# w_out loaded eight rows to a partition, with strided weights for the d products and new transfer costs in the planner

## The chip, the cores and the metric

The kernel runs on one core of a Trainium2 chip. The metric is the device time of one execution in microseconds; lower is better. Times are medians over runs. A profile is one further execution, and its rows are microseconds from the first instruction unless marked ns.

## The reference

Eight sequences of 3072 tokens go through a gated attention without softmax, and its result goes through a layer with a maximum of two products:

```python
B, S, D = 8, 3072, 256        # z has 64 columns
scores = (z @ z.transpose(0, 2, 1)) / S
attn   = np.maximum(scores, 0.0) ** 2
x      = (u * (attn @ v)).reshape(B * S, D)
h1, h2 = x @ w1, x @ w2       # w1, w2: 256 x 1024
g      = np.maximum(h1, h2)
out    = g @ w_out            # w_out: 1024 x 256
```

All inputs and the output are float32. The kernel multiplies in bf16.

## The kernel before

**Algebra.** max(h1, h2) is written as relu(x(w1 - w2)) + x w2. So the kernel computes d = x(w1 - w2), then g = relu(d), and the output as g w_out + x (w2 w_out). The small product w2 w_out, called W2o, is made once on the chip: w2 is transposed by TensorE (job `w2t`, line 1593), copied, and multiplied with w_out (job `w2o`). w1 - w2 is made once by VectorE in w1's own tile (`w1_sb`).

**Steps.** A step is 512 tokens of one sequence, so there are 6 steps to a sequence and 48 in all. The first three are "plain"; the others use a seven-product scheme (after Strassen) for the attention times v (parts X and Y), for which sums of blocks (`es`) and of v (`lf`, the "folds") are formed on VectorE. For 44 of the steps the output product uses seven products too, with sums of w_out's blocks (`wf_sb`) and of g's (`gs`). Scores are symmetric: a block is computed once, and its other use gets it by a transposing DMA (`turn`, tile `aT`; within a diagonal group, inside `a_sb`). These are issued from SyncE's queue, as are the transposes of u (`uT`) and z (`zT`) and the stores. u, v, z and the weights are loaded, and cast to bf16, by DMAs from GpSimd's queue, each set to start when a named product has run ("timed load").

**TensorE's work.** Most products are "halved": a product over 128 rows is issued as two over 64 rows each, to the two halves of the array, which run side by side. One weight load (LDWEIGHTS) precedes each. A d part (`da`, `db`) is two pairs of halves, each with 512 columns of xT streaming past 128 columns of w1 as the weights. All matmuls go through one helper and show line 86. The 1024 columns of w1 are eight blocks of 128: block i gives rows of g that meet block i of w_out's rows. Which 128 columns make a block is free, as long as w1, w2 and w_out agree on it.

**Order.** The order of TensorE's instructions is written out by hand in a list (`work`), with the scores laid between. The orders of VectorE, ScalarE, SyncE and GpSimd, and the buffers that tiles share, come from a planner that runs when the kernel is built: a greedy simulation (`find_orders`) in which each job has a cost, and takes the engine when it is ready and due. It is repeated for 24 rounds, with margins added where TensorE would have waited, and the best round is kept. Nothing of the planner runs on the chip; a job that the plan puts too early on an in-order engine makes that engine wait.

**The planner's DMA.** A transfer starts 870 ns (SyncE) or 1770 ns (GpSimd) after its issue or when the queue is free, holds the queue for its cost in `DMA` times a factor, and lands some time later (`settle`). The factor is 1.1 before 100 us of the plan and 0.9 later. The time to land is 1330 ns, and 4000 ns after 125 us except for zT. The first loads have landing times of their own (`FIRST_LOADS`) and take no place in the queue. SyncE is taken for free again 1450 ns after an issue, or 4500 ns before the queue is free, if that is later.

Of the kernel before, what the change touches and what calls it, by code (L numbers as in the profile page):

```python
# [11 lines left out]
def kernel(  # L12
# [17 lines left out]
    nc = tc.nc  # L30
# [9 lines left out]
    P = 128  # L40
# [7 lines left out]
    KF = Dff // P  # L48
# [30 lines left out]
    pin = tc.keep_in_program_order  # L79
# [5 lines left out]
    def matmul(*args, **kw):  # L85
        newest[0] = pin(nc.tensor.matmul(*args, **kw)).ins  # L86
        for ins in fence:
            tc.add_manual_dep(newest[0], ins.name, SYNC, reason="a bank's other half of rows")
        fence.clear()
# [8 lines left out]
    def halved(half, out_ap, weights, moving, start, stop, **kw):  # L98
        rows = ds(half * 64, 64)
        matmul(out_ap, weights[rows], moving[rows], start=bool(start), stop=bool(stop), **kw)  # L100

    def sp_dma(**kw):
        pin(nc.sync.dma_start(**kw))


    def load(timed=False, **kw):
        dma = pin(nc.gpsimd.dma_start(**kw))
        if timed:
# [4 lines left out]
                reason="timed load",  # L113
            )

    def make_zT(z_sb):
        zT = zpool.tile([P, NSB + 1, P], bf16, name="zT")
        flat = z_sb.rearrange("p t d -> p (t d)")
        sp_dma(out=zT[:, 0 : NSB + 1 : 2, :], in_=flat, transpose=True)
        sp_dma(out=zT[:, 1 : NSB + 1 : 2, :], in_=flat[:, ds(dqk, NSB * dqk)], transpose=True)  # L120
        return zT
# [32 lines left out]
    w1_sb = consts.tile([P, KD, Dff], bf16)  # L154
    w_out_sb = consts.tile([P, KF, D], bf16)
# [7 lines left out]
    q = seqs[0]  # L163
# [6 lines left out]
    ident = consts.tile([P, P], bf16)  # L170
# [32 lines left out]
    RELU_BIAS, SQUARE_BIAS = 1200, -300  # L203
    TURN, TURN_LAG, UT_LAG = 1750, 4000, 7000

    DMA = dict(turn=1180, uT=1130, zT=4220, store=1940, v=1680, u=1680, z=3130, w1=4100, w2=3000, wo=4500)
    DMA_SMALL, DMA_PART, DMA_FULL, DMA_FULL_TO = 970, 0.9, 1.1, 100000
    DMA_START, DMA_END, DMA_LATE, DMA_AHEAD, SP_ISSUE = {"SP": 870, "POOL": 1770}, 1330, 4000, 4500, 1450
    FIRST_LOADS = {("v", 0, 0): 0, ("v", 0, 1): 1200, ("v", 0, 2): 2500, ("v", 0, 3): 3700, ("v", 0, 4): 4900, ("v", 0, 5): 7700, ("u", 0): 6300}

    class Job:
        def __init__(self, key, ways, fn, deps, new, uses, after, lag):
# [4 lines left out]
            self.due = 1e12  # L219
            self.dma = DMA.get(key[0], 0) if "SP" in ways or "POOL" in ways else 0  # L220
            if key[0] == "turn" and key[2] is None:
# [16 lines left out]
    def tile_of(pool, key):  # L238
        return bufs[pool, key].tile
# [520 lines left out]
    def acc_buf(i, key):  # L760
        buf(f"acc{i}", key, lambda: acc_psum.tile([P, GW], fp32, name=f"acc{i}"))
# [311 lines left out]
    def add_second(st, split):  # L1073
        n, b, c = st.n, st.b, st.s
# [16 lines left out]
        for i in range(KF // 2):  # L1091


            spare = (n, i) in SPARE_D
            turn_of = len(steps) + (SPARE_D.index((n, i)) if spare else 0)
            if spare:
                for j in range(2):
                    acc_buf(j, (turn_of, 0))
            banks = [(f"acc{j}", (turn_of, 0)) for j in range(2)] if spare else [("mm", ("d", n, i))]

            def bank(j, banks=banks):
                return tile_of(*banks[j]) if len(banks) > 1 else tile_of(*banks[0])[:, j, :]

            def products(_, i=i, bank=bank):
                for j in range(2):
                    for kc in range(KD):
                        matmul(
                            bank(j),
                            w1_sb[:, kc, ts(2 * i + j, P)],
                            tile_of(*xT)[:, :, kc, :],  # L1110
                            start=(kc == 0),
                            stop=(kc == KD - 1),
                        )

            def halves_of(part, i=i, bank=bank):
                if part:
                    fence.append(marks.pop(("d", n, i)))
                for kc in range(KD):
                    for half in range(2):
                        j = half ^ part  # L1120
                        halved(
                            half,
                            bank(j),
                            w1_sb[:, kc, ts(2 * i + j, P)],
                            tile_of(*xT)[:, :, kc, :],
                            start=kc == 0 and not part,
                            stop=kc == KD - 1 and part == 1,
                        )
                if not part:
                    marks["d", n, i] = mark()  # L1130

            d_key = ("d", n, i)
            if st.parted:
                d_key = ("db", n, i)
                job(
                    ("da", n, i),
                    {"PE": 430},
                    lambda _, f=halves_of: f(0),
                    deps=st.xT_jobs + [("w1-w2",)],
                    new=banks,  # L1140
                    uses=[xT] + banks,
                    lag=150,
                )
            job(
                d_key,
                {"PE": 430 if st.parted else 864},
                (lambda _, f=halves_of: f(1)) if st.parted else products,
                deps=st.xT_jobs + [("w1-w2",)],
                new=None if st.parted else banks,
                uses=[xT] + banks,  # L1150
                lag=150,
            )

            def do_relu(eng, i=i, banks=banks, bank=bank):
                if len(banks) > 1:
                    for j in range(2):
                        relu(eng, g_at(2 * i + j)[:, 0, :], bank(j))
                else:
                    relu(eng, g_at(2 * i, 2), tile_of(*banks[0]))

            job(
                ("g", n, i),
                {"ACT": 1000} if spare else {"DVE": RELU["DVE"]} if (n, i) == (last, KF // 2 - 1) else RELU,
                do_relu,
                deps=[d_key],
                new=gs[i // 2] if i % 2 == 0 else None,
                uses=[gs[i // 2]] + banks,
                after=[("g", n, 0)] if i else (),
            )
# [48 lines left out]
        for i in range(G // per):  # L1218
# [34 lines left out]
            if split:  # L1253
# [3 lines left out]
                    lambda _, i=i: sp_dma(out=out_b[:, c * G + i, :], in_=tile_of(*ok)[:, i, :]),  # L1257
# [123 lines left out]
    for name in "s20 a10 s21 b10 a11 a12 b11 a13 s22 b12 b13 s23 a00 a01 s10 b00 b01 s11 a02 a03 b02 b03 s12 o00 s13 o01 o02 o03".split():  # L1381
        n, i = last - int(name[1]), int(name[2])
# [68 lines left out]
    for n in range(PLAIN, len(steps)):  # L1451
        i = first_of[n]
# [12 lines left out]
    for w in reversed(range(len(windows))):  # L1465
        limit = min([limit] + [due[r] for r in windows[w] if r in due])
        found = [i for i in spots if begins[i] <= limit]
        i = found[-1] if found else 0
# [108 lines left out]
    W2, W2T = ("T", "w2"), ("T", "w2T")  # L1577
    bufs[W2] = Buf(lambda tag: widepool.tile([P, KD, Dff], bf16, name="w2_sb", tag=tag))
    bufs[W2T] = Buf(lambda tag: widepool.tile([P, KD, KF, P], bf16, name="w2T_sb", tag=tag))
    for tile_sb, source, key, at, new, rows in (  # L1580
        (lambda: tile_of(*W2), moe_w2, "w2", (0, 7), W2, "(c p) f -> p c f"),
        (lambda: w1_sb, moe_w1, "w1", (1, 2), None, "(c p) f -> p c f"),
        (lambda: w_out_sb, moe_w_out, "wo", (2, 2), None, "(c p) d -> p c d"),
    ):

        def fetch(_, tile_sb=tile_sb, source=source, rows=rows):
            load(timed=True, out=tile_sb(), in_=source.rearrange(rows, p=P))

        job((key,), {"POOL": 2000}, fetch, new=new, after=at_step(0, *at), lag=6500)
    def w2_transposes(_):  # L1590
        for dc in range(KD):
            for nb in range(KF):
                pin(nc.tensor.transpose(tile_of("mm", ("w2t", 0))[:, dc, nb, :], tile_of(*W2)[:, dc, ts(nb, P)], ident))  # L1593

    job(("w2t",), {"PE": 900}, w2_transposes, deps=[("w2",)], new=("mm", ("w2t", 0)), uses=[W2], lag=150)
    for dc in range(KD):
# [3 lines left out]
            lambda eng, dc=dc: copy(eng, tile_of(*W2T)[:, dc], tile_of("mm", ("w2t", 0))[:, dc]),  # L1600
# [36 lines left out]
    for dc in range(KD):  # L1637
# [3 lines left out]
            lambda eng, dc=dc: copy(eng, W2o_sb[:, dc, :], tile_of("mm", ("w2o", dc))[:, 0, :D]),  # L1641
# [9 lines left out]
    for args in plain_todo:  # L1651
        st, i, ks, dcs = args
# [126 lines left out]
    def find_orders():  # L1779
# [3 lines left out]
        dma_free = [10000]  # L1783
# [10 lines left out]
        def settle(j, begin, ns):  # L1794
            j.begin, j.done = begin, begin + ns + j.lag
            if j.key in FIRST_LOADS:
                j.done = FIRST_LOADS[j.key]
            elif j.dma:

                dma_free[0] = max(dma_free[0], begin + DMA_START["SP" if "SP" in j.ways else "POOL"]) + (DMA_FULL if begin < DMA_FULL_TO else DMA_PART) * j.dma  # L1800
                j.done = dma_free[0] + (DMA_LATE if begin > 125000 and j.key[0] != "zT" else DMA_END)
                if "SP" in j.ways:
                    idle_from["SP"] = max(begin + SP_ISSUE, dma_free[0] - DMA_AHEAD)
            for nxt, _ in j.succ:
                nxt.waits -= 1
                if not nxt.waits:
                    release(nxt)
# [21 lines left out]
        while len(emitted) < len(jobs) - len(HEAD_JOBS):  # L1829
            best = None  # L1830
            for e, todo in ready.items():
# [7 lines left out]
                at, _, j = min(found, key=lambda x: x[:2])  # L1839

                if e != "PE":
                    near = [x for x in found if x[0] <= at + PATIENCE]
                    at, _, j = min(near, key=lambda x: x[1] + WAIT_COST * (x[0] - at))
# [3 lines left out]
            at, e, j = best  # L1847
# [155 lines left out]
```

## Time and profile before

| what | value |
|---|---|
| median of 3 runs | 894.88 us (894.75 to 896.99) |
| profiled execution | 893.2 us, span 891.4 us |
| mean granted TensorE clock | 0.998 |
| TensorE busy | 882.7 us, 99% of the span |
| VectorE, ScalarE busy | 802.4 us (90%), 757.9 us (85%) |
| DMA moved | 146.17 MB, 164 GB/s on average |
| w_out's load, issue to landing | 8.5 us, 512 KB |

The profiled execution's time is its span and what lies around it. A matmul's end is modelled in the profile, so start-to-start distances are better than durations for what a product costs. In a row of the groups the columns are: line, engine, operation, output tile and input tiles, shape, count, then busy us, mean ns of one, and the engine's idle time before them with what ended it. In the order of time they are start, length, and the instruction; idle time before it stands in brackets.

### The profile page before, as it was taken

The numbers are of one execution on the slowest core, as the hardware profiler recorded it, in microseconds if no ns is written. First come the engines' busy times: TensorE is split into PE (matmuls) and PEld (weight loads), VectorE is DVE, ScalarE is ACT, GpSimd is POOL, SyncE is SP. The second block draws the span as 40 slices with busy tenths as digits, with TensorE's granted clock in tenths as the row PEclk, the third lists the DMA queues.
The fourth block names the chain that finished last, engine by engine and source line by source line (L and its number), as shares of the span: only waits on it lengthen the run. The fifth ranks groups of instructions, "written<-read, shape, count | busy, mean of one in ns | idle before, by whom it ended". The sixth has DMA issues, their size and how long they took to land.

```text
span 891.4 us, 37531 instructions
## 1 busy us (share of the span) xinstructions
PE 882.7 (99%) x16501; PEld 738.0 (83%) x16501; DVE 802.4 (90%) x1720; ACT 757.9 (85%) x952; POOL 59.8 (7%) x127
## 2 busy tenths in 40 slices
PE   9999999999999999999999999999999999999998
PEld 3368888878889988888888878888888898888886
DVE  6867799989999999999999999989998999989985
ACT  8867998879988999789997899978999799997634
POOL 3100000000000000000000000000000010000000
PEclk9999999999999999999999999999999999999999
DMA  9999999999999989999899999999999999996722
GB/s 160 171 167 148 188 199 160 179 188 187 157 163 169 193 151 174 170 179 203 121 169 173 191 184 143 169 166 213 150 148 172 187 199 158 136 199 115 128 58 73
DMA packets 380853, 146.17 MB, mean 164 GB/s; under 512 B 359184, under 2 KB 360848, under 8 KB 380688
## 3 DMA queue, kind: packets, MB, share of 16 engines
q1 hardware_dynamic: 364128, 114.01, 79.3%
q0 software_dynamic: 16560, 29.74, 23.3%
q8 instruction: 129, 2.11, 1.0%
q14 instruction: 36, 0.29, 0.1%
HBM read 59.77 MB, written 25.17 MB: 95 GB/s over the span
## 4 chain that ended last, share of the span: by engine, by line
PE 93%; ACT 3%; DMA 1%; DVE 1%; issue 1%; POOL 0%
PE acc L86 48%; PE s_ps L86 46%; ACT a_sb L282 1%; DMA aT<-a_sb 1%; ACT g_sb L282 1%; ACT o_sb L282 0%; DMA o_sb<-in_z_dram 0%; ACT g_last L282 0%; DVE gs L299 0%; DVE gs L296 0%; ACT a_sb L288 0%; ACT w2T_sb L293 0%; PE w2t_ps L1593 0%; DVE e L296 0%; DVE a_sb L290 0%
## 5 line engine op out<-in xcount | busy, mean ns | idle before, releaser
L86 PEld LDWEIGHTS <-v_sb 64*128 64x128 bf16 (+1 forms) x4464 | 332.4, 94 | 62.2 <-issue 8.4
L282 ACT ACTIVATE a_sb<-s_ps 128x1024 bf16<-128x1024 f32 (+1 forms) x335 | 302.3, 941 | 36.5 <-PE s_ps L86 33.6
L86 PEld LDWEIGHTS <-lf 64*128 64x128 bf16 x3240 | 264.2, 94 | 16.2 <-POOLq L94 3.2
L86 PE MATMUL acc<-es,v_sb 64*128 64x256 bf16 x2160 | 274.9, 269 | 0.0
L86 PE MATMUL acc<-es,lf 64*128 64x256 bf16 x1080 | 245.0, 269 | 0.0
L86 PE MATMUL acc<-a_sb,lf 64*128 64x256 bf16 x1224 | 232.1, 269 | 0.0
L86 PE MATMUL s_ps<-xT,w_sb 64*128 64x512 bf16 (+1 forms) x1504 | 212.6, 376 | 0.1
L288 ACT ACTIVATE a_sb<-a_sb 128x1024 bf16<-128x1024 bf16 (+1 forms) x224 | 209.9, 966 | 1.5
L282 ACT ACTIVATE g_sb<-s_ps 128x1024 bf16<-128x1024 f32 x187 | 186.0, 1024 | 14.0 <-PE s_ps L86 12.0
L86 PE MATMUL acc<-aT,lf 64*128 64x256 bf16 x936 | 177.5, 269 | 2.0 <-DMA aT<-a_sb 2.0
L86 PE MATMUL acc<-a_sb,v_sb 64*128 64x256 bf16 (+1 forms) x1344 | 140.2, 279 | 0.4 <-DVE xT L303 0.2
L86 PE MATMUL s_ps<-zT 64*128 64x512 bf16 (+2 forms) x774 | 120.2, 334 | 1.0 <-DVE zT L130 0.4
L86 PEld LDWEIGHTS <-gs 64*128 64x128 bf16 x2816 | 103.3, 94 | 9.9 <-issue 0.7
L296 DVE TENSOR_TENSOR es<-aT 128x1536 bf16<-128x1536 bf16 (+1 forms) x117 | 106.2, 931 | 0.5
L86 PEld LDWEIGHTS <-w_sb 64*128 64x128 bf16 (+1 forms) x1520 | 78.2, 94 | 25.5 <-POOLq L94 1.5
L86 PEld LDWEIGHTS <-g_sb 64*128 64x128 bf16 x2304 | 87.7, 94 | 10.4 <-POOLq L94 7.3
L290 DVE TENSOR_TENSOR a_sb<-a_sb 128x1024 bf16<-128x1024 bf16 (+1 forms) x112 | 72.2, 648 | 22.7 <-ACT a_sb L282 22.6
L86 PE MATMUL acc<-aT,v_sb 64*128 64x256 bf16 x936 | 86.8, 270 | 0.0
L299 DVE TENSOR_TENSOR es<-a_sb 128x512 bf16<-128x512 bf16 x198 | 79.4, 419 | 8.2 <-PE acc L86 8.0
L86 PE MATMUL s_ps<-wf_sb,gs 64*128 64x128 bf16 x2112 | 85.6, 217 | 0.0
L296 DVE TENSOR_TENSOR es<-a_sb 128x1024 bf16<-128x1024 bf16 x108 | 72.7, 684 | 0.0
L86 PE MATMUL s_ps<-w_out_sb,g_sb 64*128 64x128 bf16 (+1 forms) x1600 | 72.6, 222 | 0.0
(94 smaller groups left out, 1101.4 us busy)
## 6 DMA issues: line engine op xcount, KB each, us to landing
out_dram<-o_sb SPq DMA_DIRECT2D x47, 512.0 KB, 4.9
v_sb<-in_v_dram POOLq DMA_DIRECT2D x48, 256.0 KB, 5.8
u_sb<-in_u_dram POOLq DMA_DIRECT2D x48, 256.0 KB, 5.0
aT<-a_sb SPq DMA_TRANSPOSE x228, 5.1
z_sb<-in_z_dram POOLq DMA_DIRECT2D x7, 384.0 KB, 6.3
w_sb<-in_moe_w_dram POOLq DMA_DIRECT2D x2, 512.0 KB, 6.7
uT<-u_sb SPq DMA_TRANSPOSE x48, 5.2
a_sb<-a_sb SPq DMA_TRANSPOSE x45, 5.6
```

Of the source, the lines that this page charges most:

```text
L86: newest[0] = pin(nc.tensor.matmul(*args, **kw)).ins
L282: pin(nc.scalar.activation(out_ap, in_ap, AF.Relu))
L288: pin(nc.scalar.activation(ap, ap, AF.Square))
L290: pin(nc.vector.tensor_mul(ap, ap, ap))
L296: pin(nc.vector.tensor_add(*args))
L299: pin(nc.vector.tensor_sub(*args))
```

## The change

w_out's 1024 rows are dealt to the partitions differently: partition p gets rows 8p to 8p + 7, which lie one behind the other in memory, instead of row p of each block of 128. Block n of w_out then holds the rows 8q + n. So the columns of w1 and w2 that make block n are 8q + n too: the view `by_place` picks every eighth column, and the d products and the transposes of w2 read their weights with a step of 8 elements (16 bytes). Shapes, counts and order of the products stay.

In the planner, w_out's queue cost is 3000 ns instead of 4500. For jobs that begin between 31 and 56 us of the plan (from the third step into the fourth) the factor is 0.8 instead of 1.1, and the time to land 2800 ns instead of 1330. After 125 us, v's loads are reckoned to land 5500 ns after their queue time instead of 4000. The first transpose of u gets a landing time of its own, 13000 ns, and so takes no queue time in the plan.

```diff
+    def by_place(tile_sb):
+        return tile_sb.rearrange("p c (q n) -> p c n q", n=KF)
...
-    DMA = dict(turn=1180, uT=1130, zT=4220, store=1940, v=1680, u=1680, z=3130, w1=4100, w2=3000, wo=4500)
+    DMA = dict(turn=1180, uT=1130, zT=4220, store=1940, v=1680, u=1680, z=3130, w1=4100, w2=3000, wo=3000)
...
-    FIRST_LOADS = {..., ("v", 0, 5): 7700, ("u", 0): 6300}
+    FIRST_LOADS = {..., ("v", 0, 5): 7700, ("u", 0): 6300, ("uT", 0): 13000}
...
                         matmul(
                             bank(j),
-                            w1_sb[:, kc, ts(2 * i + j, P)],
+                            by_place(w1_sb)[:, kc, 2 * i + j, :],
...
                         halved(
                             half,
                             bank(j),
-                            w1_sb[:, kc, ts(2 * i + j, P)],
+                            by_place(w1_sb)[:, kc, 2 * i + j, :],
...
-        (lambda: w_out_sb, moe_w_out, "wo", (2, 2), None, "(c p) d -> p c d"),
+        (lambda: w_out_sb, moe_w_out, "wo", (2, 2), None, "(p c) d -> p c d"),
...
-                pin(nc.tensor.transpose(tile_of("mm", ("w2t", 0))[:, dc, nb, :], tile_of(*W2)[:, dc, ts(nb, P)], ident))
+                pin(nc.tensor.transpose(tile_of("mm", ("w2t", 0))[:, dc, nb, :], by_place(tile_of(*W2))[:, dc, nb, :], ident))
...
-                dma_free[0] = max(dma_free[0], begin + DMA_START["SP" if "SP" in j.ways else "POOL"]) + (DMA_FULL if begin < DMA_FULL_TO else DMA_PART) * j.dma
-                j.done = dma_free[0] + (DMA_LATE if begin > 125000 and j.key[0] != "zT" else DMA_END)
+                dma_free[0] = max(dma_free[0], begin + DMA_START["SP" if "SP" in j.ways else "POOL"]) + (0.8 if 31000 < begin < 56000 else DMA_FULL if begin < DMA_FULL_TO else DMA_PART) * j.dma
+                j.done = dma_free[0] + (DMA_LATE + 1500 * (j.key[0] == "v") if begin > 125000 and j.key[0] != "zT" else 2800 if 31000 < begin < 56000 else DMA_END)
```

More of the change, by code (lines that the diff above doesn't have):

```diff
@@ L204 @@
     TURN, TURN_LAG, UT_LAG = 1750, 4000, 7000
-    DMA = dict(turn=1180, uT=1130, zT=4220, store=1940, v=1680, u=1680, z=3130, w1=4100, w2=3000, wo=4500)
+    DMA = dict(turn=1180, uT=1130, zT=4220, store=1940, v=1680, u=1680, z=3130, w1=4100, w2=3000, wo=3000)
     DMA_SMALL, DMA_PART, DMA_FULL, DMA_FULL_TO = 970, 0.9, 1.1, 100000
     DMA_START, DMA_END, DMA_LATE, DMA_AHEAD, SP_ISSUE = {"SP": 870, "POOL": 1770}, 1330, 4000, 4500, 1450
-    FIRST_LOADS = {("v", 0, 0): 0, ("v", 0, 1): 1200, ("v", 0, 2): 2500, ("v", 0, 3): 3700, ("v", 0, 4): 4900, ("v", 0, 5): 7700, ("u", 0): 6300}
+    FIRST_LOADS = {("v", 0, 0): 0, ("v", 0, 1): 1200, ("v", 0, 2): 2500, ("v", 0, 3): 3700, ("v", 0, 4): 4900, ("v", 0, 5): 7700, ("u", 0): 6300, ("uT", 0): 13000}
     class Job:
```

## The prediction

> **What bounds the kernel now.** I read the page first, for which engine sets the end.
>
> ```profile
> span 891.4 us, 37531 instructions
> PE 882.7 (99%) x16501; PEld 738.0 (83%) x16501; DVE 802.4 (90%) x1720; ACT 757.9 (85%) x952; POOL 59.8 (7%) x127
> PE 93%; ACT 3%; DMA 1%; DVE 1%; issue 1%; POOL 0%
> ```
>
> TensorE is busy for 99% of the span and holds 93% of the chain that ended last. A change that leaves its instructions as they are can only win back time in which TensorE waits or runs slowly. The waits of TensorE alone, and the windows by ten microseconds, say how much of that there is. In the waits the columns are the sum, the number and the longest; the other entries of TensorE's list are under 0.5 us each and lie before 24 us.
>
> ```profile
> PE acc L86 <- DMA aT<-a_sb: 2.0, 1, 2.0
> PE zeros L86 <- DVE blank L166: 1.2, 1, 1.2
> ```
>
> The windows list each engine's busy time, then the granted clock, the DMA share and GB/s.
>
> ```profile
> 180.00:190.00 10.00, 9.02 (x182) 8.02 (x178) 9.76 (x19) 8.58 (x12) 0.53 (x1) 1.00 1.32 173
> 190.00:200.00 10.00, 9.01 (x156) 7.72 (x157) 5.92 (x13) 6.38 (x9) 0.53 (x1) 0.83 1.15 214
> ```
>
> Behind the first two microseconds there is one wait worth naming: a transposed tile (aT) came late once, by 2.0 us. In the window behind it the granted clock is 0.83 instead of 1.00. So (1 - 0.83) x 10 = 1.7 us more went to a slow clock. The order of time shows both, and the chain shows what they did to the step.
>
> ```profile
> 176.21 0.24 PE L86 MATMUL s_ps<-xf_sb,xs 64*128 64x128 bf16 x2
> 190.99 0.29 PE L86 MATMUL acc<-aT,lf 64*128 64x256 bf16 x2 [1.97 <-DMA aT<-a_sb]
> 192.47 0.35 PE L86 MATMUL s_ps<-xf_sb,xs 64*128 64x128 bf16 x2
> ```
>
> The chain, as start, length and what ran:
>
> ```profile
> 175.03 2.84 PE s_ps L86 x56
> 182.68 8.27 DMA aT<-a_sb
> 196.76 2.84 PE s_ps L86 x56
> 286.72 2.84 PE s_ps L86 x56
> 304.66 2.84 PE s_ps L86 x56
> ```
>
> From 175.03 to 196.76 this step of the second sequence takes 21.73 us. The same step of the third, from 286.72 to 304.66, takes 17.94. The difference, 3.79 us, is 1.97 us of waiting, about 1.7 of slow clock and 0.1 of rest: the same product lasts 0.24 us before and 0.35 after. By the Trainium skill (TensorE: Matmul & The Clock Gate, HAM oscillation), idle gaps matter only above about 3.4 us; by that rule the stall would be worth 1.97 us and its end would give 892.9 us. The trace disagrees, a gap of 1.97 us was followed by the clock of 0.83, so this rule gets no chance of its own.
>
> I take 3.79 us for the whole stall.
>
> Why was that tile late? First SyncE's queue (start, length of the issue), then the DMA issues of 172 to 182 us and of 287 to 300 us, with the median time to landing.
>
> ```profile
> 153.48 13.19 SPq L103 DMA_TRANSPOSE aT<-a_sb  x6
> 177.89 1.57 SPq L103 DMA_TRANSPOSE aT<-a_sb  x1
> 179.56 3.03 SPq L103 DMA_TRANSPOSE a_sb<-a_sb  x1
> 182.68 5.71 SPq L103 DMA_TRANSPOSE aT<-a_sb  x2
> 288.60 4.15 SPq L103 DMA_TRANSPOSE aT<-a_sb  x2
> ```
>
> ```profile
> aT<-a_sb SPq DMA_TRANSPOSE x2, 9.4
> v_sb<-in_v_dram POOLq DMA_DIRECT2D x2, 256.0 KB, 8.6
> aT<-a_sb SPq DMA_TRANSPOSE x4, 6.3
> v_sb<-in_v_dram POOLq DMA_DIRECT2D x1, 256.0 KB, 4.8
> ```
>
> From 153.48 on six transposes are issued without a pause, in 13.19 us. The two issued from 182.68 have their counterpart in the third sequence at 288.60. Counted from the step's start it is 7.65 us there (182.68 - 175.03) against 1.88 (288.60 - 286.72): here the queue is 5.8 us further behind. Transfers also land later: of those issued in 172 to 182 us aT takes 9.4 us and v 8.6, in 287 to 300 us 6.3 and 4.8. The transposes ahead in the queue cost 1.57 and 3.03 us each to issue. The stall is 2.0 us deep, so one place in this queue makes or ends it.
>
> **The change part by part.** *w_out's load.* The first row below is of the two loads of w1 and w2, the second of w_out's load; then the rows of that load and its readers.
>
> ```profile
> DMA to landing us min/median/max: 6.1/6.7/7.2
> w_out_sb<-in_moe_w_out_dram POOLq DMA_DIRECT2D x1, 512.0 KB, 8.5
> 40.67 0.92 POOL L107 DMA_DIRECT2D w_out_sb<-in_moe_w_out_dram  x1 [12.55 <-PE acc L86]
> 55.17 1.95 PE L86 MATMUL s_ps<-w_out_sb,w2T_sb 128*128 128x256 bf16 x16
> L296 DVE TENSOR_TENSOR wf_sb<-w_out_sb x1: 418/418/418, 56.3 to 56.3; 128x512 bf16<-128x512 bf16 x1
> ```
>
> It moves the same 512 KB in 8 KB runs instead of 1 KB runs. w1 and w2 have the same size and runs of 4 KB; they land in 6.7 us against 8.5. I take 6.7 for the changed load (bounds 6.1 and 8.5; longer than 8.5 is excluded, as the longer runs of w1 and w2 are faster). It lands about 47.4 instead of 40.67 + 8.5 = 49.2. Its first reader on TensorE starts at 55.17, its first on VectorE at 56.3, so 6 us of slack hide both values: 0 us on the path. With the cover gone, it would be worth 1.8 us. The transfers behind it in the queue (u at 41.58, the transposes, z) gain up to the same 1.8 us; TensorE's list of waits has none between 24 and 189 us, so that too is 0 at that place. The wf sums and all products keep their shapes: 0.
>
> *Strided weights.* The d products read w1 with a step of 8 elements (16 bytes) between columns; so do the 16 transposes of w2. By the code every weight load of the kernel before reads neighbouring columns, so no row shows this price, and it needs bounds.
>
> ```profile
> L86 PEld LDWEIGHTS <-w_sb 64*128 64x128 bf16 x1504 | 76.7, 94 | 23.5 <-POOLq L94 1.5 <-issue 0.6
> 175.99 0.40 PE L86 MATMUL s_ps<-wf_sb,gs 64*128 64x128 bf16 x8
> 176.83 1.04 PE L86 MATMUL s_ps<-xT,w_sb 64*128 64x512 bf16 x8
> 177.69 0.27 PE L86 MATMUL acc<-es,v_sb 64*128 64x256 bf16 x1
> 50.45 1.06 PE L1593 MATMUL w2t_ps<-ident,w_sb 128*128 128x128 bf16 x16
> 51.34 3.94 PE L86 MATMUL s_ps<-xT,w_sb 128*128 128x512 bf16 x16
> ```
>
> Eight products of 128 columns run from 175.99 to 176.21: 4 pairs in 0.22 us, 55 ns a pair. Each pair has two weight loads of its own, so two loads take at most 55 ns of the engine, whatever the 94 ns of a single record. A d pair streams 512 columns: from 176.83 to 177.69, 4 pairs in 0.86 us, 215 ns. Inside d the loads may become 215 / 55 = 3.9 times as long before anything waits. The thin place is the first pair of a d part that follows an output part, whose pairs cover only 55 ns: by the order of work that is 3 places in each of 44 steps, 132. At a double load each shows up to 55 ns: 132 x 55 ns = 7.3 us. The 16 transposes, at (51.34 - 50.45) / 16 = 56 ns each, add at most 0.9 us. Over 3.9 times as long, d itself would wait as well; no row points there, and the range leaves it out. Bounds: 0 and 8.2 us; a gain is excluded, since the loads of today already show nothing to win. I take 0, because the row it is nearest to is d's own, with its 160 ns of spare cover.
>
> The Trainium skill has rules for both sides. SBUF — State Buffer (Door 1, the note on cachelines) gives lines of 16 bytes and a price for each access to a new line; with this step every weight is on a new line, which speaks for the 7.3 us. TensorE: Matmul & The Clock Gate (Weight-path perf modes) lets the fast weight load take steps up to 1,024 elements, which speaks for 0. No run here shows either.
>
> *The plan's numbers.* TensorE's order comes from the list of work and is not touched. GpSimd's loads hang on products of that order and stay where they are. The orders of VectorE, ScalarE and SyncE, and which tile takes which buffer, come from the plan, and it reckons anew. The plan's zero is the first product.
>
> ```profile
> 7.69 1.02 PE L86 MATMUL acc<-a_sb,v_sb 128*128 128x512 bf16 x4
> aT<-a_sb SPq DMA_TRANSPOSE x228, 5.1
> 181.46 0.42 DVE L296 TENSOR_TENSOR lf<-v_sb 128x512 bf16<-128x512 bf16 x1
> 173.59 0.53 POOL L107 DMA_DIRECT2D v_sb<-in_v_dram  x1 [3.01 <-PE s_ps L86]
> ```
>
> So 31 to 56 us of the plan is 38.7 to 63.7 in the trace. There w_out was reckoned at 1770 + 1.1 x 4500 + 1330 = 8050 ns and becomes 1770 + 0.8 x 3000 + 2800 = 6970; a transpose goes from 870 + 1.1 x 1180 + 1330 = 3498 to 870 + 944 + 2800 = 4614, nearer to the 5.1 us of the trace. The queue is believed free 2550 ns earlier behind w_out and 354 ns earlier per transpose, so SyncE's order may differ from there on. After 125 us of the plan (133 in the trace) a v load goes from 1770 + 0.9 x 1680 + 4000 = 7282 to 8782 ns. The measured 8.6 us of the stalled stretch is nearer to the new number. It matters there: the first fold of v starts at 181.46, 7.87 us after its load was issued at 173.59 and in front of squares, on which transposes wait. The four folds (0.42 us each, 1.7 us together) move behind such work. New waits are not added to the code; an instruction placed too late holds up all behind it on its in-order engine, and TensorE then waits for an es or aT tile.
>
> The sum: w_out 0, strided loads 0, head of the kernel 0 (written by hand, unchanged), the stall -3.79. The profiled execution takes 893.2 us (its span and 1.8 around it) and would take 889.4; the median of the runs, 894.88, lies 1.7 above it and gives 894.88 - 3.79 = 891.1.
>
> **The rivals.** *A, the stall goes* (forecast): 891.1. For it: only 2.0 us of lateness, one place in SyncE's queue; both reckonings come nearer to what landed, the one for v just in this stretch. Against: the transposes ahead of the late one are probably ready earlier in any order.
>
> *B, the stall stays as it is*: 894.9. For it: SyncE issues without a pause for long before 182.68, so the 1.8 us saved at 49 us may be used up on the way.
>
> *C, another order, one more late tile*: DMA share is above 1 in the windows shown, so the queue has no spare time; if a plan with less queue time puts one more transpose (1.57 to 3.03 us of issue) ahead of one that is due, TensorE gets a second stall like this one. Price 3.79: 894.88 + 3.79 = 898.7. It decides as soon as the second tile is late by some tenths of a us.
>
> *D, strided loads show*: 894.88 + 7.3 = 902.2, 898.4 if the stall goes as well. It decides when two loads take over 55 + 2700 / 132 = 75 ns.
>
> **How the numbers follow.** A 0.52, B 0.16, C 0.20, D 0.12. About 0.3% (2.7 us) is what a measurement can tell from no change, so A is faster, B the same, C and D slower: 0.52, 0.16, 0.32. A's own range is 889.0 (the stall worth 1.7 us more in the runs that weren't profiled, and some tenths) to 892.2. The range over the cases is 889.0 to 901.0: it takes in A, B and C, and leaves out D's upper part, C with two more stalls and a little below, under 0.2 in all.
>
> **What would show it.** A: TensorE's waits without the 2.0 us for aT, a clock of 1.00 in 190 to 200 us, 17.9 us for that step. w_out's landing near 6.7 us, and TensorE contiguous from 40 to 58 us. Strided loads: 4 d pairs still in 0.86 us; 0.22 us more at the first pair after an output part would be D. C: a new entry "DMA aT" or "DVE es" in TensorE's waits and another window with a clock under 1.00. The forecast is wrong if the wait at 189 us is there still, or if one like it stands elsewhere.

## The result, and the profile after

The change makes the kernel slower: 900.95 us (median of 21, 894.24 to 905.56) against 894.59 before (median of 21, 891.85 to 900.04). The ratio is 1.0053, with a 95% interval of 1.0030 to 1.0077. That is half a percent. Measured three times more, the same kernel gave 1.0017 (0.9995 to 1.0039), 1.0031 (0.9992 to 1.0070) and 1.0053 (1.0026 to 1.0079); two of these intervals contain 1. The ratios leave out slow executions, those over 1.5% above the fastest of their kernel, while medians and counts here take all (without the slow ones the two counts below are 22 of 58 and 22 of 175).

The median hides the shape. The 21 times lie in two groups: ten from 894.24 to 896.79, with mean clocks of 0.999 to 1.000, and eleven from 900.95 to 905.56, with 0.996 to 0.998. I draw the line at 899 us and count the executions above it; in later measurements the two groups run into each other there (e16 has times of 898.24 and 899.61). Over all the measurements told of here they are 22 of 58 for the changed kernel and 24 of 177 for the kernel before (its single execution e12 not counted). So there are two questions: what makes an execution fall above the line, and what the lower group costs.

The profiled execution of the changed kernel took 895.05 us and fell in the lower group. Its page:

```profile
span 893.2 us, 37530 instructions
PE 884.3 (99%) x16501; PEld 766.2 (86%) x16501; DVE 800.8 (90%) x1719; ACT 759.4 (85%) x953; POOL 59.4 (7%) x127
PE 92%; ACT 4%; DVE 2%; issue 1%; DMA 1%; POOL 0%; POOLq 0%
```

TensorE still sets the end. Its instructions are as many as before; the weight loads (PEld) are busy for 28 us longer. The waits of TensorE (sum, number, longest; "issue" is a wait for which the profile shows no cause):

```profile
PE acc L86 <- issue: 1.3, 3, 0.5
PE zeros L86 <- DVE blank L169: 1.2, 1, 1.2
PE tpz_c L132 <- DMA z_sb<-in_z_dram: 0.6, 1, 0.6
PE s_ps L86 <- issue: 0.3, 1, 0.3
PE s_ps L86 <- DVE o_sb L299: 0.3, 1, 0.3
```

The windows that answer to the stall of before (busy time of each engine, granted clock, DMA share, GB/s):

```profile
180.00:190.00 10.00, 10.00 (x199) 9.73 (x196) 9.46 (x20) 9.21 (x12) 0.83 (x2) 1.00 1.29 209
190.00:200.00 10.00, 10.00 (x199) 9.51 (x196) 9.47 (x22) 9.26 (x15) 1.29 (x3) 1.00 1.06 174
```

The wait for aT is gone, TensorE is full from 180 to 200 us, and the clock is 1.00 throughout. That is what case A asked for, and the span is still 1.8 us longer than in the profile of before. The kernel before, profiled a second time (e12: 892.24 us, span 890.4, clock 1.000), shows why nothing was won:

```profile
180.00:190.00 10.00, 10.00 (x200) 9.13 (x197) 9.65 (x20) 9.21 (x11) 0.53 (x1) 1.00 1.27 216
190.00:200.00 10.00, 10.00 (x202) 8.87 (x198) 9.53 (x22) 9.41 (x15) 1.58 (x3) 1.00 1.09 188
```

The stall at 189 us isn't there either, and e1, which has the orders of before, doesn't have it (its longest wait is 1.5 us, at 735 us). It belonged to one execution of the kernel before, not to the kernel. Nor does its absence show in full: the span of e12 is only 1.0 us shorter than that of the profile with the stall. Among other things, e12 has 2.1 us of "issue" waits that the other has not.

**Where an upper execution loses.** One profile of the changed kernel fell above the line (904.58 us, span 902.7; experiment e16). The two longest waits of TensorE in it, behind the head:

```profile
PE acc L86 <- DMA a_sb<-a_sb: 6.0, 1, 6.0
PE acc L86 <- DVE e L299: 0.9, 1, 0.9
```

The windows around the first:

```profile
55.00:60.00 5.00, 4.08 (x49) 3.03 (x48) 2.04 (x5) 2.64 (x5) 0.53 (x1) 1.00 1.61 74
60.00:65.00 5.00, 0.00 (x0) 0.00 (x0) 0.00 (x0) 0.00 (x0) 0.00 (x0) 0.79 1.04 148
65.00:70.00 5.00, 4.90 (x50) 4.08 (x50) 3.59 (x12) 0.00 (x0) 0.00 (x0) 0.52 1.26 187
```

TensorE stands still for 6.0 us at 59 to 65 us, until the transposed diagonal tile of the fourth step (`turn` 3) lands. The five microseconds behind that run at 0.52 of the clock, worth (1 - 0.52) x 5 = 2.4 us. With the 0.9 us for e this is 9.3 of the 9.5 us by which its span exceeds the 893.2 of the lower execution.

**How it got there.** SyncE's queue (start, length of the issue) in the kernel before:

```profile
34.01 1.39 SPq L103 DMA_TRANSPOSE uT<-u_sb  x1
46.21 1.21 SPq L103 DMA_TRANSPOSE a_sb<-a_sb  x1
66.95 3.85 SPq L103 DMA_TRANSPOSE a_sb<-a_sb  x1
```

in the lower profile of the changed kernel:

```profile
36.97 1.29 SPq L103 DMA_TRANSPOSE uT<-u_sb  x1
39.54 10.24 SPq L103 DMA_TRANSPOSE aT<-a_sb  x4
49.88 1.43 SPq L103 DMA_TRANSPOSE a_sb<-a_sb  x1
73.97 1.24 SPq L103 DMA_TRANSPOSE a_sb<-a_sb  x1
```

and in the upper one:

```profile
38.38 1.29 SPq L103 DMA_TRANSPOSE uT<-u_sb  x1
39.76 13.72 SPq L103 DMA_TRANSPOSE aT<-a_sb  x4
53.58 4.51 SPq L103 DMA_TRANSPOSE a_sb<-a_sb  x1
```

The new plan puts transposes that are due later in front: `turn` 1-16 and 1-18 ahead of the third step's uT, 2-16 and 2-18 as well ahead of the diagonal tile, and seven more ahead of the next diagonal tile (`turn` 4). The first diagonal tile is issued at 49.88 instead of 46.21, the second at 73.97 instead of 66.95. With quick transfers that is early enough. In the upper execution the four transposes ahead take 13.72 us to issue instead of 10.24, and the tile itself takes 11.5 us to land instead of 5.2. The length of an issue holds its waiting too. The longest wait of SyncE's queue from 39 to 54 us, first in the upper execution, then its wait for TensorE in the lower one:

```profile
SPq L103 <- PE acc L86: 7.0, 1, 7.0
SPq L103 <- PE s_ps L86: 4.2, 1, 4.2
```

Both belong to `turn` 2-16, one of the transposes put in front: it isn't ready to go, and the diagonal tile stands behind it. The DMA issues of 40 to 64 us (median us to landing) in the lower profile:

```profile
w_out_sb<-in_moe_w_out_dram POOLq DMA_DIRECT2D x1, 512.0 KB, 6.3
u_sb<-in_u_dram POOLq DMA_DIRECT2D x2, 256.0 KB, 7.1
a_sb<-a_sb SPq DMA_TRANSPOSE x1, 5.2
```

and in the upper one:

```profile
w_out_sb<-in_moe_w_out_dram POOLq DMA_DIRECT2D x1, 512.0 KB, 9.2
u_sb<-in_u_dram POOLq DMA_DIRECT2D x2, 256.0 KB, 9.4
a_sb<-a_sb SPq DMA_TRANSPOSE x1, 11.5
```

Program and data are the same in both; what differs from execution to execution is how fast the early transfers land.

In the kernel before, the same tile lands no faster:

```profile
a_sb<-a_sb SPq DMA_TRANSPOSE x1, 10.2
```

It takes 10.2 us there, 10.4 in e12 and 12.3 in e4, and it is in time each time, because it is issued at 46.21 to 46.81: in e4 TensorE has no wait over 0.2 us from 24 to 100 us. Against the profile of before the upper execution issues the tile 7.4 us later (53.58 against 46.21), and its landing takes only 1.3 us more.

### The profile page after: what moved, and what is told of

Read it like the earlier page. It is cut to its first block, busy times and chain, and to the rows that moved or that the text cites. A ratio compares the mean times of both kernels' runs of the same rounds, so it can differ in the third digit from the quotient of the medians.

```text
span 893.2 us, 37530 instructions
## 1 busy us (share of the span) xinstructions
PE 884.3 (99%) x16501; PEld 766.2 (86%) x16501; DVE 800.8 (90%) x1719; ACT 759.4 (85%) x953; POOL 59.4 (7%) x127
## 4 chain that ended last, share of the span: by engine, by line
PE 92%; ACT 4%; DVE 2%; issue 1%; DMA 1%; POOL 0%; POOLq 0%
PE acc L86 47%; PE s_ps L86 45%; ACT a_sb L285 1%; ACT g_sb L285 1%; ACT a_sb L291 1%; DMA z_sb<-in_z_dram 1%; ACT o_sb L285 0%; DVE lf L302 0%; ACT e L820 0%; DVE o_sb L299 0%; DVE es L302 0%; DVE a_sb L293 0%; DVE o_sb L302 0%; DVE gs L302 0%; DVE gs L299 0%
## 5 line engine op out<-in xcount | busy, mean ns | idle before, releaser
L86 PEld LDWEIGHTS <-v_sb 64*128 64x128 bf16 (+1 forms) x4464 | 336.8, 94 | 58.0 <-issue 9.5
L86 PEld LDWEIGHTS <-lf 64*128 64x128 bf16 x3240 | 268.0, 94 | 14.1 <-DVE lf L302 1.2
L86 PE MATMUL s_ps<-xT,w_sb 64*128 64x512 bf16 (+1 forms) x1504 | 217.0, 378 | 0.2
L291 ACT ACTIVATE a_sb<-a_sb 128x1024 bf16<-128x1024 bf16 x225 | 210.9, 966 | 1.6
L86 PE MATMUL acc<-aT,lf 64*128 64x256 bf16 x936 | 179.4, 269 | 0.5 <-issue 0.5
L86 PE MATMUL s_ps<-zT 64*128 64x512 bf16 (+2 forms) x774 | 123.4, 333 | 1.0 <-DVE o_sb L299 0.3
L86 PEld LDWEIGHTS <-w_sb 64*128 64x128 bf16 (+1 forms) x1520 | 107.6, 142 | 12.9 <-issue 0.7
```

The lines of the kernel that those rows point to most:

```text
L291: pin(nc.scalar.activation(ap, ap, AF.Square))
```

## The experiments

Each ratio is to the kernel before, measured beside it on the same chip, with its 95% interval. "Plan" means the planner's numbers, "layout" the new w_out with the strided weights.

**The change taken apart: e1, e2, e3, e4.** e1 is the layout with the planner's numbers of before. e2 is the planner's numbers with the old layout. e3 is the whole change again. e4 is the kernel before with one of the numbers:

```diff
-                j.done = dma_free[0] + (DMA_LATE if begin > 125000 and j.key[0] != "zT" else DMA_END)
+                j.done = dma_free[0] + (DMA_LATE + 1500 * (j.key[0] == "v") if begin > 125000 and j.key[0] != "zT" else DMA_END)
```

> The layout alone (w_out eight rows to a partition, strided weights), with all planner numbers of before, so the orders of all engines are those of before. Theory O (the new orders make a tile late in part of the executions): 894.6 + 129 d parts behind an output part x 7.5 ns = 895.6 us, the wait of 2.0 us for aT at 189 us still there, times in one group. Theory W (strided weight loads cost the time): about 900 us as with the whole change.

> The planner numbers alone, with w_out in blocks of 128 rows and weights of neighbouring columns as before. Theory O: two groups of times as with the whole change, one near 893 to 895 us and one near 902 to 905 us, since the orders are those of the change. Theory W: 890 to 892 us, the stall at 189 us gone and nothing in its place.

> The whole change once more. Both theories: two groups of times, near 895 and near 903 us. If the profiled execution falls in the upper group: theory O expects one or two waits of TensorE of 2 us or more for an aT or es tile, each followed by a granted clock under 1.00; theory W expects no such wait but longer d parts.

> The kernel before with one number changed: v's loads after 125 us of the plan land 1500 ns later in the plan. Theory O with v's number as the cause: the wait at 189 us gone, 891 us in a lower group, and an upper group 8 us above it. Theory O with the early numbers as the cause: about 894.6 us, one group. Theory W: 891 to 895 us.

Measured: e1 893.38 us (0.9997, 0.9981 to 1.0012), none of 12 above 899. e2 901.50 (1.0066, 1.0035 to 1.0097), 8 of 12. e3 896.22 (1.0017), 2 of 13. e4 895.43 (1.0007, 0.9989 to 1.0026), none of 12. So the plan's orders make the loss, and neither the layout nor the later v does. No run changes another of the planner's numbers alone, so which of them moves the transposes stays open. Beside each other on one chip, the plan alone does worse than the whole change (e2 8 of 12, e3 2 of 13 above 899; over all runs 18 of 24 and 22 of 58). With the old layout w_out took 8.5 us or more to land in every profile, with the new one 6.2 to 7.1 in the quick ones, so the faster load may give back some lead; that isn't shown. e3's profile (906.45 us) fell above the line, at another place than e16's. Its waits from 44 to 72 us:

```profile
ACT w2T_sb L296 <- DVE w2T_sb L296: 10.9, 1, 10.9
PE s_ps L86 <- ACT w2T_sb L296: 10.1, 1, 10.1
DVE xT L306 <- DMA uT<-u_sb: 8.8, 1, 8.8
```

SyncE's issue of the third step's uT, as start and length:

```profile
51.06 5.45 SPq L103 DMA_TRANSPOSE uT<-u_sb  x1
```

The loads of w1 and of the third step's u (issues of 29.2 to 34 us, with the us to landing):

```profile
w_sb<-in_moe_w_dram POOLq DMA_DIRECT2D x1, 512.0 KB, 16.2
u_sb<-in_u_dram POOLq DMA_DIRECT2D x1, 256.0 KB, 17.0
```

The longest wait of SyncE's queue from 39 to 52 us:

```profile
SPq L103 <- DVE a_sb L293: 8.0, 1, 8.0
```

And the windows:

```profile
60.00:65.00 5.00, 0.00 (x0) 0.00 (x0) 2.71 (x6) 0.79 (x1) 0.00 (x0) 0.50 1.12 213
65.00:70.00 5.00, 4.72 (x22) 2.58 (x22) 4.90 (x13) 4.34 (x6) 0.00 (x0) 0.66 0.94 181
```

w1 took 16.2 us to land and the third step's u 17.0. That u was issued at 29.39, so it was there at 46.4. Its uT was issued at 51.06 only, instead of 36.97: in front of it stand `turn` 1-16 and 1-18, and the first of them waited 8.0 us for a tile of VectorE, which had itself waited 3.4 us for an aT that landed late. Late transfers and the new order work together here. VectorE waits 8.8 us for uT with the product xT. VectorE is in order, so its copy of w2T stands behind. ScalarE waits for that copy, and TensorE for ScalarE's. In the window behind, the clock is 0.66.

**Two transposes forward or back: e5 to e8.** Theory Q: the third step's uT and the diagonal tile of the fourth, put behind transposes that are not due, make the upper group. e5 is the plan again. e6 and e7 are plan and whole change with these two in front again; e8 is the kernel before with the two moved back.

```diff
+    put_behind(('uT', 2), [('turn', 1, 16), ('turn', 1, 18)])             # e6, e7
+    put_behind(('turn', 3, None), [('turn', 2, 16), ('turn', 2, 18)])
...
+    put_behind(('turn', 2, 12), [('uT', 2)])                              # e8
+    put_behind(('turn', 2, 18), [('turn', 3, None)])
```

> The planner numbers alone once more, as the measure of this call. Both theories: about 901 us, two thirds of the executions over 899 us.

> The planner numbers alone, and in SyncE's queue two urgent transposes taken back in front of two that are not: uT of the third step before turn (1,16) and (1,18), and the diagonal turn of the fourth step before turn (2,16) and (2,18). Nothing else of the orders changes. Theory Q (these two places in the queue make the upper group): about 894 us, hardly an execution over 899 us. Theory R (another part of the new orders, such as VectorE's folds that wait for v, makes it): 900 us or more, as without the edit.

> The whole change with the same two transposes taken back in front. Theory Q: 894 to 895 us, no execution over 899 us. Theory R: 896 to 901 us with a tenth to a half of the executions over 900 us, as for the whole change.

> The kernel before with the two transposes moved back in SyncE's queue: uT of the third step behind turn (1,16) and (2,12), the diagonal turn of the fourth step behind uT of that step and turn (1,18), (2,16) and (2,18). Theory Q: an upper group near 900 to 906 us appears, median 897 to 903 us. Theory R: 894.5 us as before.

Measured: e5 901.14 us (1.0058, 1.0020 to 1.0096), 10 of 12 above 899. e6 894.33 (1.0024, 0.9983 to 1.0065), 4 of 12. e7 902.08 (1.0061, 1.0024 to 1.0098), 7 of 12. e8 899.52 (1.0058, 1.0027 to 1.0089), 8 of 12. Moving the two back is enough to spoil the kernel before. Moving them forward helps the plan (4 of 12 against 10 of 12 in e5) and doesn't help the whole change (e7). The profile of e8 (903.47 us) has the stall of e3: TensorE waits 8.2 us at 54 us, through w2T, for the third step's uT. The profile of e7 (waits of TensorE) shows what was left there:

```profile
PE s_ps L86 <- ACT w2T_sb L296: 5.2, 1, 5.2
PE acc L86 <- DMA a_sb<-a_sb: 4.6, 1, 4.6
```

The first is the third step's uT again, which stands in front now, but waits for its u (12.8 us to land) and then takes 15.1 us itself. The second wait ends at 95.7 us, at the second diagonal tile, which the new plan also puts back and which I hadn't moved.

**The whole early queue: e9 to e12.** Theory Q2: all of SyncE's early order counts. e9 is the whole change a third time. e10 is the whole change with the first 32 issues of SyncE in the order of before. e11 is the layout with `turn` 0-18 and 1-16 put behind the diagonal tile. e12 is one profiled execution of the kernel before.

```diff
+    lines["SP"] = [named[k] for k in queue_of_before] + [x for x in lines["SP"] if x[0].key not in queue_of_before]    # e10
...
+    put_behind(('turn', 3, None), [('turn', 0, 18), ('turn', 1, 16)])     # e11
```

> The whole change, as the measure of this call. All theories: 896 to 902 us, a sixth to a half of the executions over 899 us.

> The whole change, but the first 32 jobs of SyncE's queue (about the first 95 us) in the order of the kernel before; VectorE, ScalarE, TensorE and GpSimd keep the orders of the change. Theory Q2 (the early order of SyncE's queue as a whole makes the upper group, not the two places alone): median 893.5 to 895.5 us, at most a sixth of the executions over 899 us, as for the kernel before. Theory R (VectorE's order or the weights): as the whole change in this call.

> The layout alone with the planner numbers of before (893.38 us when it was measured), and in SyncE's queue turn (0,18) and (1,16) moved behind the diagonal turn of the fourth step, so that uT of the third step and three more urgent ones go ahead of them. Theory Q2: at or under 893.4 us, no execution over 898 us. Theory R: 893.4 us with executions up to 900 us, as the queue's early order would not matter.

> The kernel before once more, for a second profile. By theory Q2 the slow loads of the first 60 us, seen in four of the nine profiles of changed kernels (w1 landing after 12 us and more), come to this kernel as well, and cost it little: if this profile has them, TensorE waits under 3 us before 60 us; if it has not, the wait for aT of 2.0 us at 189 us is probably not there again.

Measured: e9 896.92 us (1.0031), 3 of 12 above 899. e10 897.52 (1.0032, 0.9997 to 1.0067), 1 of 12: fewer than the 3 of e9, though 12 executions can't tell these apart, and the lower group stands at 897.4 (median of the 11), so my 893.5 to 895.5 was missed. The one above the line is the profiled one (907.63 us); it waits 3.6 us for an aT at 103 us, behind the 32 issues that were put back. e11 896.85 (1.0022, 0.9987 to 1.0057), 4 of 12: no gain. e12 is the 892.24 us shown above.

**Is the queue's order enough: e13 to e16.** Theory Q3: the early order by itself makes the upper group; rival R: the rest of the new plan. e13 is the kernel before with the new order of SyncE's first 32 issues, e14 the plan with the old order, e15 and e16 are e10 and the whole change again.

> The kernel before with the new plan's order in the first 32 issues of SyncE alone; layout, weights, GpSimd's loads and the other engines' orders stay. Theory Q3 (the order of SyncE's early issues by itself makes the upper group): at least half of the executions lie above 899 us, most of them with a clock of 0.998 or less, and the median is 898 to 902. Rival R (the rest of the new plan, its other order of GpSimd's loads and of the later transposes, makes it): at most 3 in 12 above 899 as in the kernel before (13 of 98 so far), and a median of 893.5 to 896.

> The new planner numbers on the old layout, with the first 32 issues of SyncE in the order of the kernel before. Theory Q3: the share above 899 us falls from 18 of 24 (the planner numbers alone, two runs) to at most 2 in 12, median 893 to 896. Rival R: more than half stay above 899 us, median 899 to 902.

> The whole change with the first 32 issues of SyncE in the order of the kernel before, once more. Theory Q3: as the first time, at most 2 in 12 above 899 us, and the others at 895 to 898, so that a median of 2 to 3 us over the kernel before remains, which the order does not explain (1.0 us of it from the strided weights). Rival R: as the whole change beside it, a third or more above 899 us.

> The whole change once more, beside the others on one chip. Theory Q3: a third to two thirds of the executions above 899 us (13 of 34 so far), the rest at 894 to 897; the median falls into either. Rival R the same, but then the run with the old order of the queue beside it shows the same share.

Measured: e13 894.79 us (1.0010, 0.9980 to 1.0039), 2 of 12 above 899. e14 895.62 (1.0013, 0.9986 to 1.0039), 2 of 12. e15 896.84 (1.0041, 1.0019 to 1.0064), 3 of 12. e16 898.93 (1.0053), 6 of 12. Neither theory holds: the old order mends the new plan (2 of 12 in e14 against 18 of 24 in e2 and e5, on other chips), but the new order doesn't spoil the kernel before.

**What is the other half: e17, e18.** In the new plan GpSimd loads w1 ahead of the third step's u. Theory U: that is the other half. e17 puts u in front again in the plan; e18 gives the kernel before both the new order of SyncE and w1 ahead of u.

```diff
+    at_u, at_w = (next(i for i, x in enumerate(lines["POOL"]) if x[0].key == k) for k in (("u", 2), ("w1",)))
+    lines["POOL"][at_u], lines["POOL"][at_w] = lines["POOL"][at_w], lines["POOL"][at_u]
```

> The new planner numbers on the old layout, with one thing put back: on GpSimd's queue the load of u for the third step stands in front of w1 again, not behind it. SyncE's order stays the new one. Theory U (two halves are needed: SyncE's new order, in which all that follows waits behind the third step's uT, and u behind w1, which makes that uT late when the loads are slow): the share above 899 us falls from 18 of 24 to at most 4 in 12, median 893.5 to 897. Rival V (SyncE's new order with any other part of the new plan): more than half above 899 us, median 899 to 902.

> The kernel before with both halves of the new plan's early order and no more: SyncE's first 32 issues in the new order, and w1 in front of u for the third step on GpSimd's queue. Theory U: at least half above 899 us (SyncE's order alone: 2 of 12), median 898 to 902. Rival V: at most 3 in 12 above 899 us, median 893.5 to 896.

Measured: e17 901.53 us (1.0050, 1.0015 to 1.0086), 8 of 12 above 899. e18 894.25 (0.9985, 0.9952 to 1.0018), none of 12. Theory U falls on both sides. The profile of e18 (895.94 us) does have the stall at the first diagonal tile, issued at 51.14 with 10.2 us to land, but only 1.9 us of it. e17's profile (span 900.0) waits for the second diagonal tile, at 82 to 87 us. TensorE's wait:

```profile
PE acc L86 <- DMA a_sb<-a_sb: 4.9, 1, 4.9
```

The window around its end, with a clock of 0.62:

```profile
85.00:90.00 5.00, 2.92 (x26) 2.27 (x27) 2.42 (x6) 0.39 (x2) 0.34 (x1) 0.62 1.18 260
```

Executions above 899 us, of all:

| | SyncE's early order of before | SyncE's early order of the new plan |
|---|---|---|
| the rest of the plan as before | 24 of 177 (before), 0 of 12 (e1), 0 of 12 (e4) | 2 of 12 (e13), 0 of 12 (e18) |
| the rest of the plan new | 6 of 36 (e10, e14, e15) | 48 of 94 (whole change 22 of 58, plan 18 of 24, e17 8 of 12) |

The versions with a partly moved order are not in the table: 4 of 12 (e6), 7 of 12 (e7), 8 of 12 (e8) and 4 of 12 (e11). The nine profiles of changed versions above the line show where TensorE waited. "w2T" is the wait for the third step's uT, as in e3. The last column is the granted clock at and behind the stop.

| profile | us | longest waits of TensorE | granted clock |
|---|---|---|---|
| e2 | 901.69 | 2.6 us at 59 us, first diagonal tile; 1.9 and 1.4 us for e at 101 and 112 us | 1.0 |
| e3 | 906.45 | 10.1 us at 55 us, w2T | 0.5 for 10.2 us |
| e5 | 899.80 | 3.8 us at 82 us, second diagonal tile | 1.0 |
| e6 | 905.41 | 5.5 us at 54 us, w2T; 4.0 us at 89 us, second diagonal tile | 0.5 for 3.4 us, twice |
| e7 | 911.93 | 5.2 us at 55 us, w2T; 4.6 us at 91 us, second diagonal tile | 0.5 for 6.8 us and for 3.4 us |
| e8 | 903.47 | 8.2 us at 54 us, w2T | 0.5 for 10.2 us |
| e10 | 907.63 | 3.6 us at 103 us, an aT | 0.5 for 6.8 us |
| e16 | 904.58 | 6.0 us at 59 us, first diagonal tile | 0.5 for 6.8 us |
| e17 | 901.72 | 4.9 us at 82 us, second diagonal tile | 0.5 for 6.8 us |

Shown: the new plan makes the loss, the profiles above the line stall at transposes that land late, and with the rest of the plan new the early order of before takes most of the upper group away (6 of 36 against 48 of 94). The cells of the table come from several chips; for the whole change alone, the pairs measured beside each other have 4 of 24 with the old order (e10, e15) and 9 of 24 with the new (e9, e16), which would not settle it. Open: which part of the rest the new order needs. It isn't the place of w1. What is left are the orders of VectorE and ScalarE, which make the tiles that SyncE transposes, the buffers that tiles share, GpSimd's order of the first loads of v, and SyncE's order behind its 32nd issue. Open as well is why e8, whose order is close to e13's, rises to 8 of 12. Its profile had slow loads (w1 13.7 us), those of e13 and e18 quick ones (6.7 and 6.5), so no profile shows e13's order under slow loads.

## Why the prediction was wrong, step by step

**The stall of 3.79 us: the step that failed first.** Its size was read rightly from its profile, and it does go away. But it was a property of one execution: the second profile of the kernel before has no such wait and a clock of 1.000. So "894.88 - 3.79" took away from the median what the median hadn't in it. The step from the profiled execution to the median rested on nothing but a difference of 1.7 us between the two.

**Nothing between 24 and 189 us: the step that made it slower.** The sum put the head of the kernel at 0 as unchanged, and the transfers behind w_out at 0 because TensorE has no wait from 24 to 189 us in the profile of before. It also took GpSimd's loads to stay where they are; in the changed kernel w1 goes ahead of the third step's u. The longest stalls of all nine profiles above the line lie in just this stretch, at 54 to 103 us. In e16 the waits there and the low clock cost 9.3 us where the sum has 0.

**Case C, another order with late tiles: right in kind, wrong in size and chance.** It named the mechanism (a plan that believes in less queue time puts transposes ahead of one that is due) and then priced it as one small stall, 3.79 us, with a chance of 0.20. The longest stalls in the nine profiles above the line are 2.6 to 10.1 us of waiting, in eight of them at one of three places (the third step's uT, the first or the second diagonal tile), and in seven of the nine the clock fell as well. The upper group holds 22 of 58 executions. The forecast asked only whether the late tile of one profile becomes punctual. It didn't ask how much lead the moved transposes had left if transfers land later than in that profile.

**What the plan reckons.** I held the change's 0.8 for a better number because it came nearer to the landing times. For the order it can work the other way: by the planner's code, a queue that is believed free sooner lets SyncE take tiles that are ready before tiles that are due. That this number moved the transposes is argued from the code; no run changes it alone.

**w_out's load.** Forecast 6.7 us; measured 6.3 us in the lower profile, and up to 12.9 in an upper one. 0 on the path, as forecast: in the lower profile TensorE has no wait over 0.3 us from 24 to 127 us.

**Strided weights: forecast 0, about 1 us by the traces.** The records grew by half (the row of before had 94 ns); the page's group:

```profile
L86 PEld LDWEIGHTS <-w_sb 64*128 64x128 bf16 (+1 forms) x1520 | 107.6, 142 | 12.9 <-issue 0.7
```

The products of one step in the order of time:

```profile
176.34 1.11 PE L86 MATMUL s_ps<-xT,w_sb 64*128 64x512 bf16 x8
178.31 0.38 PE L86 MATMUL s_ps<-xT,w_sb 64*128 64x512 bf16 x1
178.40 1.03 PE L86 MATMUL s_ps<-xT,w_sb 64*128 64x512 bf16 x7
179.19 0.27 PE L86 MATMUL acc<-es,v_sb 64*128 64x256 bf16 x1
```

The same step begins in the profile of before with this row, and its last, the product for X behind the second d part, starts at 177.69:

```profile
174.85 1.04 PE L86 MATMUL s_ps<-xT,w_sb 64*128 64x512 bf16 x8
```

From the first d part (176.34) to the product behind the second (179.19) are 2.85 us, and 2.84 before (177.69 - 174.85). The halves of a pair no longer start together: the first two of the second part start at 178.31 and 178.40, 0.09 us apart, where the trace of before has 0.02. The pairs behind them keep their pace of 0.22 us. Over all starts of both traces, a d part that follows an output part takes 7 to 9 ns longer until the next product starts (medians of 439 to 440 for 432 ns, 872 for 863); behind other parts it takes no longer. There are some 130 such places: 8 ns x 130 = 1.0 us as an estimate, far under case D's 7.3. e15 against e14 on one chip, which differ in the layout alone, agrees: the executions below 899 us have medians of 896.46 and 895.51, though single executions of one kernel lie 2 to 4 us apart. e1 shows no cost, but its interval would hide 1 us. Of the two rules of the Trainium skill that the prediction weighed, TensorE: Matmul & The Clock Gate (Weight-path perf modes) was the nearer one; no run tells whether the longer record comes from the cachelines of SBUF — State Buffer.

**The lower group.** Below the line the whole change lies 0.6 to 2.8 us over the kernel before (medians, in the four measurements; 895.98 us against 893.54 beside e9). About 1 us may be the strided weights. The cause of the rest is open: waits of "issue" as in the profile after (1.6 us in all) are there in the kernel before as well (2.1 us in e12).

**What remained of the range.** 900.95 us lies inside 889.0 to 901.0, at its end. That is luck: the median fell just into the upper group, which case C priced at 898.7, and the medians of the same kernel in e3, e9 and e16 are 896.22, 896.92 and 898.93. None of the versions tried beats the kernel before: the best, e1 and e18, have intervals that contain 1.

## What to carry to other kernels

A stall in a profile is worth subtracting only if it is there in most executions; profile the starting kernel twice before taking it as the gain. Where an in-order queue feeds an engine that is never idle, look at the lead of each transfer, from landing to first use, and not at whether it waits today: a reorder that spends the lead costs little in a quick execution and here some 6 to 10 us in one whose transfers land late. Compare distributions, not only medians, when a change moves orders.

## What the runs showed of the hardware

The time of early transfers varies much from execution to execution of one program. w1, the same 512 KB at the same place, landed in 6.3 us in one profile of the changed kernel and in 16.2 in another (e3), and the transpose of the first diagonal tile in 5.2 and in 11.5 (e16). I found no cause in the program.

The clock can fall at short stops already, but doesn't always. At the 1.97 us of the kernel before ten microseconds ran at a mean of 0.83, and by the trace the granted clock was 0.5 for 3.4 us of them; the 1.9 us of e18 did the same. Behind a stop of 6.0 us five microseconds ran at 0.52 (e16). But behind the 2.6 us of e2 and the 3.8 us of e5 the clock stayed at 1.00. So the length of a stop alone doesn't decide it here, and what does is open. In the table above every low stretch is 0.5 for 3.4, 6.8 or 10.2 us. The rule of the Trainium skill that was quoted in the prediction (TensorE: Matmul & The Clock Gate, HAM oscillation), by which gaps matter only above about 3.4 us, fits the stop of 6.0 us and neither that of 1.97 us nor that of 3.8 us. Where the clock falls, a stall costs more than its length: (6.0 + 2.4) / 6.0 = 1.4 times in e16, and 3.79 / 1.97 = 1.9 times in the kernel before.
